# Other slot order in the first half; set 1 of the tokens turned by VectorE from 512-byte pieces

## The chip, the cores and the metric

The kernel runs on one core of one Trainium2 chip. The metric is device time in microseconds (us), the median of several runs of the same program. The kernel works in fp32 values with matmuls in the fp32r format.

## The reference

Input `A_u` is `[1, 2048, 576]` in fp32: 2048 tokens with 576 features. Cut to what matters:

```python
x  = A_u
xn = _layernorm(x)                       # per token
s  = S4D(xn)                             # long convolution over the tokens, per feature
def _B_ref(x, w1, b1, w2, b2):           # per token; d_ff = 4608
    y = _layernorm(x)
    h = _gelu(y @ w1 + b1)
    return h @ w2 + b2
g  = _silu(_B_ref(xn, ...))
return x + s * g
```

S4D builds a kernel K of length 2048 for each feature from sums of complex exponentials, convolves it with `xn` through a Fourier transform and adds `xn * D_skip`. The MLP (`_B_ref`) is nearly all of the arithmetic.

## The kernel before, in words

**Accuracy by halves.** A matmul takes fp32r operands. So each operand is split into a high part (the copy that ACT writes in fp32r) and a low part (the difference, that DVE subtracts), and a product is three matmuls: high by high, high by low, low by high. This holds for the tokens (`XH`, `XL`, and `XR` for the last 64 features, high and low in one tile), the weights (`w1h`, `w1l`, `w1r`, `w1s`, `w2h`, `w2l`) and the hidden values (`hh`, `hl`).

**Slots.** The 16 tiles of 128 tokens are worked in two halves of 8, and each half in two sets of 4 tiles (512 tokens). Tile b holds the tokens b, b + 16, b + 32 and so on. The 4608 hidden units are cut into 12 groups (`NG`) of 384. A slot is one group on one set: first layer (three pieces of 128 hidden units, 14 matmuls each, contracting over the features in four blocks of 128 and one of 64), Gelu on ACT, then the second layer (72 matmuls), whose results DVE adds into `acc` (line 573). There are 48 slots, and before the change they go: group 0 set 0, group 0 set 1, group 1 set 0, group 1 set 1 and so on, twice over, once for each half. The first slot has a first layer of its own (`first_layer1`).

**Weights.** `load_raw` brings the weights of a group in pieces into the tile `raw` through SP's queue, in the order of the list `PARTS`; `split_raw` splits a piece (ACT line 488, DVE line 485) and then issues the loads of the pieces that may take its room. There is one copy of the split weights of each layer, so the next group's `w1` is split while the last slot of the present group is in its second layer, and its `w2` while the next slot is in its first; `weigh_in` queues this, with times by which each piece is due.

**Tokens.** Each tile is normalised on DVE (`norms`: `stats`, `roots`, `recip`, `second`), and its tokens must be turned so that features lie on partitions. The first half does this on PE: `y_transpose` (line 413) transposes 128 x 128 blocks of a tile into PSUM, from which ACT takes the high part (417, 419) and DVE the low part (423, 425). Set 0 is turned ahead of slot 0, set 1 by `turn_lines(4, 1)` between slots 0 and 1. The second half stores its normalised tiles to the DRAM tensor `y_s` (line 388). `block_lines` then loads them back for one block of 128 features and 512 tokens at a time, in four DMAs on SP's queue of 32 partitions each, in pieces of 32 features (128 bytes, line 1231), so that one DVE transpose of 32 x 32 blocks (line 1236) puts features on partitions; ACT (1241) and DVE (1248) split the result.

**S4D.** Beside the MLP, DVE, ACT and POOL prepare S4D's tables; its matmuls (lines 869 to 1059) are put on PE between those of the MLP. The normalised tiles for it are stored to `xn_s` by POOL.

**What sets the order.** `Order` is a planner that runs while the program is traced. It keeps a clock for each engine, with a cost written into each step, and lines of steps that wait for marks of other steps (`need`, `mark`). Steps of the MLP are urgent and have times by which they are due; others go where the planner finds an engine free. `pin` fixes the order found on each engine, SP's queue among them. On the chip an engine keeps to this order and waits where an operand isn't there, whatever the planner had thought.

Of the kernel before, what the change touches and what calls it, by code (L numbers as in the profile page):

```python
# [9 lines left out]
F32 = mybir.dt.float32  # L10
# [8 lines left out]
P = 128  # L19
# [16 lines left out]
G = 3  # L36
# [6 lines left out]
def dve(n):  # L43
    return 0.075 + 0.00104 * n
# [168 lines left out]
def mixer_kernel(ctx, tc, u, log_a_real, a_imag, c_real, c_imag, log_dt, d_skip, w1, b1, w2, b2,  # L213
# [22 lines left out]
    y_s = dr.tile([8, P, D], F32, name="y_s")  # L236
# [114 lines left out]
    def norms(b0, n):  # L351
# [31 lines left out]
        def second(t, engine=nc.vector):  # L383
# [3 lines left out]
            if b0 >= 8:  # L387
                nc.sync.dma_start(dram(y_s, (b0 + t - 8) * P * D, [[D, 64], [64 * D, 2], [1, D]]), y)
            else:
                YT[b0 + t] = y  # L390
# [14 lines left out]
    def y_transpose(b0, tb, kb, q=None):  # L405
# [6 lines left out]
        def turn(i):  # L412
            nc.tensor.transpose(q[:n, i * P:(i + 1) * P], YT[b0 + i][:, kb * P:kb * P + n], idp)  # L413
# [24 lines left out]
    def load_raw(queue=nc.sync):  # L438
# [10 lines left out]
        elif i < KB:  # L449
            queue.dma_start(r, w1[i * P:(i + 1) * P, f])  # L450
        else:
            for e in range(2):
                queue.dma_start(r[e * 64:(e + 1) * 64], w1[KB * P:, f])
# [96 lines left out]
    def layer2(g, tb, j, terms, last, alone=False):  # L550
# [5 lines left out]
        c = slice(j * P, (j + 1) * P)  # L556
        if alone and terms[0][1]:
# [12 lines left out]
        def add(dh, n):  # L570
            o = acc[:, tb * 4 + j].rearrange("p (h d) -> p h d", h=2)[:, dh:dh + n]
            b = bias2.rearrange("p (h d) -> p h d", h=2)[:, dh:dh + n]
            nc.vector.tensor_add(o, q[:, dh:dh + n, :288], b if g == 0 else o)  # L573
# [616 lines left out]
    def norm_lines(b0, n=4):  # L1190
# [6 lines left out]
        for t in range(n):  # L1197
            nl["steps"].append(step("DVE", 0.6, lambda t=t: second(t), mark=("yn", b0 + t)))
            xl["steps"].append(step("POOL", 2.6, lambda t=t: first(t), need=[("yn", b0 + t)], mark=("xs", b0 + t)))
            wx["steps"].append(step(None, 5.0, lambda: None, need=[("xs", b0 + t)], mark=("xn", b0 + t)))  # L1200

    def turn_lines(b0, tb):
        x, xh, x2 = nl, nlh, nl2
        cell = {}

        def first(k0):
            for kb in (k0, k0 + 1):
                if kb <= KB:
                    cell[kb] = y_transpose(b0, tb, kb)
                    for i in range(4):  # L1210
                        cell[kb][0](i)
        M = lambda *a: ("turn", tb, b0) + a
        for ks in ((0, 1), (2, 3), (4,)):
            x["steps"].append(step("PE", 0.5 * len(ks), lambda k0=ks[0]: first(k0), cv=1,
                                   need=[M("l", 1)] if ks[0] == KB else (), mark=M("t", ks[0])))
            for kb in ks:
                xh["steps"].append(step("ACT", 0.6, lambda kb=kb: cell[kb][1](), need=[M("t", ks[0])], mark=M("h", kb)))
            for kb in ks:
                x2["steps"].append(step("DVE", 0.6, lambda kb=kb: cell[kb][2](), cv=-(kb == ks[-1]),
                                        need=[M("h", ks[-1])], mark=("x", tb) if kb == KB else M("l", kb)))  # L1220

    YB = []

    def block_lines():

        def load(tb, kb):
            if not YB:
                YB.extend(sb.tile([P, D], F32, name="row", bufs=NROW)[:, :TB] for _ in range(4))
            y = YB[(tb + kb) % 2]
            for q in range(4 if kb < KB else 2):  # L1230
                nc.sync.dma_start(y[32 * q:32 * q + 32].rearrange("p (b j) -> p b j", j=32), dram(
                    y_s, 4 * tb * P * D + kb * P + 32 * q, [[D, 32], [32 * D, NT], [1, 32]]))

        def blocks(tb, kb):
            n, k = P if kb < KB else 64, (tb + kb) % 2
            nc.vector.transpose(YB[2 + k][:n], YB[k][:n])

        def high(tb, kb):
            y = YB[2 + (tb + kb) % 2]
            if kb < KB:  # L1240
                nc.scalar.activation(XH[:, kb, tb], y, AF.Copy)
            else:
                nc.scalar.activation(XR[:64, tb], y[:64], AF.Copy)
# [308 lines left out]
```

## Time and profile before

| What | Value |
| --- | --- |
| Median of 3 runs | 1083.9 us (1082.99 to 1084.34) |
| The profiled execution's own time | 1082.74 us |
| Its span (first to last instruction) | 1081.0 us |
| Mean granted PE clock | 0.998 |
| PE busy | 1071.7 us, 99% |
| PE weight loads busy | 933.9 us, 86% |
| DVE busy | 947.9 us, 88% |
| ACT busy | 650.7 us, 60% |
| POOL busy | 199.1 us, 18% |
| DMA | 125.54 MB, mean 116 GB/s |

PE is TensorE's matmuls, PEld its weight loads, DVE is VectorE, ACT ScalarE, POOL GpSimd and SP SyncE, which issues DMAs. L413 is line 413 of the kernel. A row of a group gives line, engine, operation, the tiles written and read, shapes and count, then the busy us, the mean ns of one, the idle time of the engine ahead of them and what ended it. A row of the timeline gives start and length in us, engine, line, operation, tiles and count. Matmuls are pipelined, so the length of one contains part of its neighbours.

### The profile page before, as it was taken

What the parts mean: (1) busy time and instruction counts of PE and PEld (TensorE: products, weight loads), DVE (VectorE), ACT (ScalarE), POOL (GpSimd) and SP (SyncE); (2) the same over time, 40 slices, a digit from 0 to 9 for tenths busy, and PEclk for the clock granted to TensorE, in tenths of its full rate; (3) what the DMA queues carried; (4) which work ended last, traced back from release to release, by engine and by line L of the source; (5) the groups of instructions that cost most, each with busy time, mean ns of one, the idle gap of its engine ahead of it and who ended that gap; (6) DMA issues with size and microseconds to landing.
All of it is one profiled execution on the core that took longest, in us unless ns stands there. A gap on an engine that the chain in (4) does not pass through costs nothing.

```text
span 1081.0 us, 27198 instructions
## 1 busy us (share of the span) xinstructions
PE 1071.7 (99%) x11491; PEld 933.9 (86%) x11491; DVE 947.9 (88%) x1518; ACT 650.7 (60%) x974; POOL 199.1 (18%) x281
## 2 busy tenths in 40 slices
PE   9999999999999999999999999999999999999997
PEld 7989999889888888888888888888888887888896
DVE  7797878989999999999999999999999996677366
ACT  6558569767666665767756666576665754233333
POOL 6559342110000200002100010000100022110231
PEclk9999999999999999999999999999999999999999
DMA  7746455823225221455523433142312347332344
GB/s 236 229 140 190 163 186 196 229 71 113 72 71 110 65 80 55 112 94 129 144 59 100 82 86 88 33 124 55 97 53 76 115 85 237 111 111 88 89 156 117
DMA packets 136537, 125.54 MB, mean 116 GB/s; under 512 B 88156, under 2 KB 108096, under 8 KB 135392
## 3 DMA queue, kind: packets, MB, share of 16 engines
q1 hardware_dynamic: 120624, 76.44, 26.2%
q0 software_dynamic: 15040, 46.40, 13.8%
q8 instruction: 90, 1.47, 0.6%
q10 hardware_dynamic: 752, 0.97, 0.3%
q14 instruction: 31, 0.25, 0.1%
HBM read 95.52 MB, written 34.01 MB: 120 GB/s over the span
## 4 chain that ended last, share of the span: by engine, by line
PE 98%; DVE 1%; issue 1%; DMA 0%; ACT 0%; POOL 0%; ACTq 0%; POOLq 0%; DVEq 0%
PE mxa L508 22%; PE mxa L565 21%; PE mxb L565 21%; PE mxb L508 21%; PE cv L869 3%; PE cv L979 3%; PE cv L1032 2%; PE cv L941 2%; PE cv L1059 1%; DMA idp<-in_ident_dram 0%; PE mxa L523 0%; PE cv L413 0%; DVE A L646 0%; DVE row L386 0%; DVE acc L573 0%
## 5 line engine op out<-in xcount | busy, mean ns | idle before, releaser
L565 PE MATMUL mxa<-w2h,hh 128*128 128x288 f32 x573 | 171.3, 299 | 0.0
L565 PE MATMUL mxb<-w2h,hh 128*128 128x288 f32 x576 | 170.9, 297 | 0.0
L565 PE MATMUL mxb<-w2h,hl 128*128 128x288 f32 x576 | 170.0, 295 | 0.0
L565 PE MATMUL mxb<-w2l,hh 128*128 128x288 f32 x576 | 169.6, 294 | 0.0
L565 PE MATMUL mxa<-w2h,hl 128*128 128x288 f32 x573 | 169.1, 295 | 0.0
L565 PE MATMUL mxa<-w2l,hh 128*128 128x288 f32 x573 | 168.7, 294 | 0.0
L547 DVE TENSOR_TENSOR hl<-h,hh 128x512 fp32r<-128x512 f32 x144 | 99.4, 692 | 76.8 <-ACT hh L544 76.1
L541 ACT ACTIVATE h<-mxa,b1t 128x512 f32<-128x512 f32 x73 | 50.2, 690 | 126.3 <-PE mxa L508 121.7
L769 POOL DMA_DIRECT2D par<-par_s x36 | 27.3, 759 | 519.4 <-DVE mg L812 479.7
L565 PEld LDWEIGHTS mxa<-w2h,hh 128*128 128x128 f32 x573 | 107.6, 188 | 9.4 <-issue 6.3
L565 PEld LDWEIGHTS mxb<-w2h,hh 128*128 128x128 f32 x576 | 108.2, 188 | 4.9 <-issue 2.5
L565 PEld LDWEIGHTS mxb<-w2l,hh 128*128 128x128 f32 x576 | 108.1, 188 | 0.6
L565 PEld LDWEIGHTS mxa<-w2l,hh 128*128 128x128 f32 x573 | 107.6, 188 | 0.7
L565 PEld LDWEIGHTS mxb<-w2h,hl 128*128 128x128 f32 x576 | 108.1, 188 | 0.0
L565 PEld LDWEIGHTS mxa<-w2h,hl 128*128 128x128 f32 x573 | 107.5, 188 | 0.0
L541 ACT ACTIVATE h<-mxb,b1t 128x512 f32<-128x512 f32 x71 | 48.9, 689 | 76.9 <-PE mxb L508 76.1
L544 ACT ACTIVATE hh<-h 128x512 fp32r<-128x512 f32 x144 | 90.8, 632 | 4.0
L573 DVE TENSOR_TENSOR acc<-mxa,acc 128x576 f32<-128x576 f32 x88 | 65.4, 743 | 17.0 <-PE mxa L565 16.7
L508 PE MATMUL mxa<-XH,w1h 128*128 128x512 f32 x284 | 80.2, 404 | 0.0
L508 PE MATMUL mxb<-XH,w1h 128*128 128x512 f32 x280 | 77.1, 397 | 0.0
L508 PE MATMUL mxa<-XL,w1h 128*128 128x512 f32 x284 | 76.2, 390 | 0.0
L508 PE MATMUL mxa<-XH,w1l 128*128 128x512 f32 x284 | 76.0, 389 | 0.0
(231 smaller groups left out, 2420.8 us busy)
## 6 DMA issues: line engine op xcount, KB each, us to landing
raw<-in_B_w_dram SPq DMA_DIRECT2D x72, 288.0 KB, 3.3
raw<-in_B_w_dram SPq DMA_DIRECT2D x96, 192.0 KB, 2.9
par_s<-A POOLq DMA_DIRECT2D x8, 1080.0 KB, 5.9
par<-par_s POOLq DMA_DIRECT2D x36, 240.0 KB, 3.3
f2t<-f2q SPq DMA_DIRECT2D x24, 256.0 KB, 3.7
raw<-in_B_w_dram SPq DMA_DIRECT2D x48, 96.0 KB, 3.6
u_s<-in_A_u_dram POOLq DMA_DIRECT2D x16, 288.0 KB, 4.3
xc<-xn_s SPq DMA_DIRECT2D x48, 96.0 KB, 3.8
```

Source lines behind the costliest of these rows:

```text
L508: nc.tensor.matmul(q, a, b, start=j == 0, stop=j == len(ops) - 1)
L541: nc.scalar.activation(t, q, AF.Gelu_apprx_tanh, bias=b1t[:, g * G + i:g * G + i + 1], scale=1.0)
L544: LAST[0] = nc.scalar.activation(hh[:, i], t, AF.Copy)
L547: nc.vector.tensor_sub(hl[:, i], t, hh[:, i].bitcast(F32))
L565: nc.tensor.matmul(q[:, dh, :288], a[:, i, c], b[:, i, d], start=i == 0 and k == 0, stop=i == G - 1 and k == 2)
L573: nc.vector.tensor_add(o, q[:, dh:dh + n, :288], b if g == 0 else o)
L769: nc.gpsimd.dma_start(PAR[b].rearrange("p (g i) k -> p g (i k)", g=4), dram(par_s, (b // 6 * CH + b % 6 * 4) * NPAR, [[D * NPAR, P], [24 * ...
L869: nc.tensor.matmul(q[32 * g:32 * g + 32, i // 2, i % 2 * 64:i % 2 * 64 + 64], U[:, ri, 4 * g + i, :], v[:, ri, 4 * g + i, :], start=ri == ...
L941: nc.tensor.matmul(Q1ST[i, x][g // 2][64 * f:64 * f + 64, g % 2].rearrange(order), f1t[r].rearrange("p s k -> p (s k)"), rhs(r, f), start= ...
L979: nc.tensor.matmul(Q[i][32 * q:32 * q + 32, f, 2 * ri:2 * ri + 2], m[r, 4 * i + q, 32 * ri:32 * ri + 32], A2[r, 4 * p + 2 * i + q // 2, :, ...
L1032: nc.tensor.matmul(QI[q // 2][64 * f:64 * f + 64, q % 2, i], MAT["g2t", p + i // 2][r, i % 2, ri], YS[p + i // 2][0][r, i % 2, ri, f], sta ...
L1059: nc.tensor.matmul(Q[f][32 * e:32 * e + 32, t], g1t[r], A2[r, k:k + 2, 1].rearrange("p i d r -> p i r d"), start=True, stop=True, skip_gro ...
```

## The change

It has three parts.

1. **Order of the slots.** The first half starts with group 0 set 0, group 1 set 0, group 1 set 1, group 0 set 1, and goes on with group 2 as before. Group 0's weights are loaded and split a second time for the fourth slot. The first sum into `acc` of a set (with the bias) is found by a list of slots instead of by group 0.
2. **Set 1 of the first half is turned by DVE.** Its four tiles are stored to `y_s` as those of the second half are, and `block_lines(0)` takes the place of `turn_lines`. Its buffers lie in a tile that is free at that time, and its steps stand first in the planner's list. The loads of x from tile 8 on now come after the fourth block's load is issued.
3. **512-byte pieces.** In `block_lines`, for both halves, a load takes one tile of 128 tokens and 512 features, in pieces of 128 features. After the transpose of 32 x 32 blocks, partition p then holds the features 4p to 4p + 3, so that block k of the contraction is every fourth feature from k on. So that this holds everywhere, `w1`'s rows are loaded with a step of four, and the PE transposes of set 0 read the tile with a step of four elements. The last 64 features are loaded as before.

The diff, cut to its core:

```diff
-            if b0 >= 8:
-                nc.sync.dma_start(dram(y_s, (b0 + t - 8) * P * D, [[D, 64], [64 * D, 2], [1, D]]), y)
+            if b0 >= 4:
+                nc.sync.dma_start(dram(y_s, (b0 + t - 4) * P * D, [[D, 64], [64 * D, 2], [1, D]]), y)
...
         def turn(i):
-            nc.tensor.transpose(q[:n, i * P:(i + 1) * P], YT[b0 + i][:, kb * P:kb * P + n], idp)
+            y = YT[b0 + i]
+            y = y[:, kb:KB * P:KB] if kb < KB else y[:, KB * P:]
+            nc.tensor.transpose(q[:n, i * P:(i + 1) * P], y, idp)
...
-    for half in range(2):
-        for g in range(NG):
-            PARTS += [(half, g, 1, i) for i in range(KB + 1)] + [(half, g, 2, i) for i in range(G)]
+    SETS = [(0, (0,)), (1, (0, 1)), (0, (1,))] + [(g, (0, 1)) for g in list(range(2, NG)) + list(range(NG))]
+    SEQ = [(n, g, tb) for n, (g, tbs) in enumerate(SETS) for tb in tbs]
+    FIRST = (0, 2, 2 * NG, 2 * NG + 1)
+    for n, (g, _) in enumerate(SETS):
+        PARTS += [(n, g, 1, i) for i in range(KB + 1)] + [(n, g, 2, i) for i in range(G)]
...
-            queue.dma_start(r, w1[i * P:(i + 1) * P, f])
+            queue.dma_start(r, dram(w1, i * F + g * G * P, [[KB * F, P], [1, n]]))
...
+            if b0 == 4:
+                od.line()["steps"].append(step(None, 3.0, lambda: None, need=[("yn", b0 + t)], mark=("ys", b0 + t)))
...
-    def turn_lines(b0, tb):
...
+    def block_lines(half=1):
+
+        YB = []
+        if half == 0:
+            YB += [A2F[:, k:k + TB] for k in (2 * D, PT0 + 4 * D, PT0 + 4 * D + TB, PT0 + 4 * D + 2 * TB, 0, D)]
...
+        def source(tb, i):
+            return (0, 1, 4, 0, 5)[i] if half == 0 else (tb + i) % 2
+
+        def load(tb, i):
...
+            y = YB[source(tb, i)]
+            r = 4 * (tb + 1 if half else 0)
+            for q in range(4 if i < KB else 2):
+                if i < KB:
+                    nc.sync.dma_start(y[32 * q:32 * q + 32].rearrange("p (b d) -> p b d", b=4), dram(
+                        y_s, (r + i) * P * D + P * q, [[D, 32], [32 * D, 4], [1, P]]))
...
+        def blocks(tb, i):
+            k = (tb + i) % 2
+            x, y = YB[2 + k], YB[source(tb, i)]
+            if i < KB:
+                nc.vector.transpose(x.rearrange("p (k b t) -> p k b t", k=4, b=4),
+                                    y.rearrange("p (b j k) -> p k b j", k=4, b=4))
...
+        ks = [(tb, i) for tb in ((1,), range(2))[half] for i in range(KB + 1)]
         for n, k in enumerate(ks):
...
+            a, b, c, d = (yl, ml, mlh, ml2) if half else [od.line() for _ in range(4)]
+            early = half == 0
+            a["steps"].append(step(None, 3.5 + 1.5 * (k[1] == KB) if early else 5.5, lambda k=k: load(*k), mark=M("yl", *k),
+                                   need=[("ys", 4 + min(n, 3))] + ([M("yt", *ks[0])] if n == 3 else []) if early else [M("yt", *ks[n - 2])] if n > 1 else []))
...
+        if early:
+            d["steps"][-1]["mark"] = "x", 1
+            od.lines = od.lines[-20:] + od.lines[:-20]
...
-    turn_lines(4, 1)
+    block_lines(0)
...
-    nl["steps"].append(step(None, 7.0, rest_of_norms))
+    nl["steps"].append(step(None, 7.0, rest_of_norms, need=[("yl0", 1, 3)]))
...
-        g, tb = slot // 2 % NG, slot % 2
-        n = slot // 2
+        n, g, tb = SEQ[slot]
+        change = slot + 1 < NSLOT and SEQ[slot + 1][0] != n
```

More of the change, by code (lines that the diff above doesn't have):

```diff
@@ L235, in mixer_kernel @@
     u_s = dr.tile([P, NT, D], F32, name="u_s")
-    y_s = dr.tile([8, P, D], F32, name="y_s")
+    y_s = dr.tile([12, P, D], F32, name="y_s")
     g_s = dr.tile([8, P, D], F32, name="g_s")
@@ L556, in layer2 @@
         c = slice(j * P, (j + 1) * P)
+        first = turn[0] - 1 in FIRST
         if alone and terms[0][1]:
@@ L572, in add @@
             b = bias2.rearrange("p (h d) -> p h d", h=2)[:, dh:dh + n]
-            nc.vector.tensor_add(o, q[:, dh:dh + n, :288], b if g == 0 else o)
+            nc.vector.tensor_add(o, q[:, dh:dh + n, :288], b if first else o)
         return add
@@ L1458, in mixer_kernel @@
                 od.advance(od.t["PE"])
-                if pos == G - 1 and tb == 1 and slot + 1 < NSLOT:
+                if pos == G - 1 and change:
                     weigh_in(1)
@@ L1490, in mixer_kernel @@
                     od.urgent.append((od.t["PE"], chain))
-                if pos == NPOS - 1 and tb == 1 and slot + 1 < NSLOT:
+                if pos == NPOS - 1 and change:
                     weigh_in(2)
```

68 lines of the change are left out of this document (23 added, 45 removed).

## The prediction

> **What bounds the kernel now.** I read the page first (busy times, the chain that ended last), then PE's own waits, then PE's timeline where the change lies.
>
> ```profile
> span 1081.0 us, 27198 instructions
> PE 1071.7 (99%) x11491; PEld 933.9 (86%) x11491; DVE 947.9 (88%) x1518; ACT 650.7 (60%) x974; POOL 199.1 (18%) x281
> PE 98%; DVE 1%; issue 1%; DMA 0%; ACT 0%; POOL 0%; ACTq 0%; POOLq 0%; DVEq 0%
> ```
>
> ```profile
> PE mxa L1117 <- POOL XL L1111: 1.3, 1, 1.3
> PE cv L413 <- DMA idp<-in_ident_dram: 0.5, 1, 0.5
> ```
>
> PE sets the end throughout. These are the two longest of its three waits (us in total, times, longest); the third has 0.2 us, and all lie ahead of the end of start-up, 13 us. After that it waits for no engine. So the time follows the work on PE: a change gains what it takes off PE, and loses every wait that it puts in. DVE comes second with 88%.
>
> ```profile
> 22.64 0.29 PE L565 MATMUL mxa<-w2h,hh 128*128 128x288 f32 x1
> ...
> 29.79 2.26 PE L413 MATMUL cv<-idp,row 128*128 128x128 f32 x16
> 31.80 0.38 PE L565 MATMUL mxb<-w2h,hh 128*128 128x288 f32 x1
> 32.02 0.30 PE L565 MATMUL mxb<-w2l,hh 128*128 128x288 f32 x1
> ...
> 34.27 0.60 PE L413 MATMUL cv<-idp,row 128*64 128x128 f32 x4
> 34.62 1.17 PE L508 MATMUL mxa<-XH,w1h 128*128 128x512 f32 x4
> 35.63 1.07 PE L508 MATMUL mxa<-XL,w1h 128*128 128x512 f32 x4
> 36.54 1.07 PE L508 MATMUL mxa<-XH,w1l 128*128 128x512 f32 x4
> ...
> 44.24 0.29 PE L565 MATMUL mxb<-w2h,hh 128*128 128x288 f32 x1
> ...
> 53.76 1.09 PE L508 MATMUL mxb<-XH,w1h 128*128 128x512 f32 x4
> ```
>
> Matmuls overlap, so the price of one is the distance from its start to the next: 0.13 us in the second layer (44.24 to 53.76 for 72), 0.91 us for four of the first (35.63 to 36.54). A slot is 34.62 to 53.76, 19.1 us, of which the second layer takes 9.5.
>
> **What comes off PE.** The 20 transposes of set 1 go. Sixteen hold PE from 29.79 to 31.80, 2.01 us; the matmul behind them holds 0.22 instead of 0.13, so 0.09 more. Four hold 34.27 to 34.62, 0.35 us; the four matmuls behind them 1.01 instead of 0.91, 0.10 more. Sum 2.01 + 0.09 + 0.35 + 0.10 = **2.55 us**. All else stays on PE: 48 slots, only in another order.
>
> **What is added on the other engines.** Group 0's weights come twice in the first half, and set 1 is turned on DVE.
>
> ```profile
> L485 DVE TENSOR_TENSOR w2l<-raw,w2h 128x576 fp32r<-128x576 f32 x72 | 50.3, 748 | 1.8 <-ACT w2h L488 1.7
> L485 DVE TENSOR_TENSOR w1l<-raw,w1h 128x384 fp32r<-128x384 f32 x94 | 47.6, 556 | 0.0
> L1043 DVE STREAM_TRANSPOSE A<-A 128x512 f32<-128x512 f32 x36 | 22.8, 682 | 1.2 <-ACT A L1039 1.2
> L1236 DVE STREAM_TRANSPOSE row<-row 128x512 f32<-128x512 f32 x8 | 5.3, 686 | 0.0
> ```
>
> ```profile
> L488 ACT ACTIVATE w2h<-raw 128x576 fp32r<-128x576 f32 x72 | 44.8, 675 | 49.9 <-PE mxa L565 48.8 <-DMA raw<-in_B_w_dram 1.0
> L488 ACT ACTIVATE w1h<-raw 128x384 fp32r<-128x384 f32 x96 | 42.2, 509 | 0.1
> ```
>
> DVE: 5 w1 splits at 0.556 and 3 w2 splits at 0.748 are 5.0 us, 5 block transposes at 0.69 are 3.4: +8.4 us. The five high and five low parts of set 1 are there before and after. ACT: 5 at 0.509 and 3 at 0.675, +4.6 us. The new transposes read every fourth element, which no row does. Bounds: 0.68 (L1043 reads pairs from far apart and costs what the plain L1236 does) and twice that; I take 0.69, from the nearest row. At twice, DVE does 3.4 us more.
>
> Set 1's work runs in the gaps that DVE and ACT have in the first slots; the S4D work behind it moves back by up to 8.4 us and has room near the end (a stretch, then the busy us of PE, PE's weight loads, DVE, ACT and POOL, each with its number of instructions, the granted clock, DMA's share and GB/s):
>
> ```profile
> 920.00:940.00 20.00, 20.00 (x183) 16.92 (x182) 9.82 (x18) 5.21 (x10) 5.07 (x10) 1.00 0.28 80
> 30.00:40.00 10.00, 9.87 (x62) 8.71 (x61) 4.93 (x8) 7.07 (x10) 8.90 (x8) 1.00 0.72 267
> ```
>
> DVE idles 10.2 of the 20 us from 920 on with PE full, and 5.1 of the 10 us from 30 on: cost 0. Without that cover, 8.4 us of S4D would stand at the end. DMA gets 1.8 MB of weights (4 x 192 + 2 x 96 + 3 x 288 KB), 1.15 MB of stores to y_s and as much of block loads: 4.1 MB, some 15 us at the 267 GB/s of the second row. The loads of x from tile 8 on, 2.3 MB, move behind them.
>
> **The new deadlines.** Slot 0's second layer starts at 22.64 and, without transposes, ends 9.5 us later, at 32.2. Slot 1 is group 1 on set 0 from 32.2 to 51.3, with its second layer from 41.8. Set 1 is due at 51.3 instead of 34.6; w1 of group 1 at 32.2 instead of 53.8.
>
> ```profile
> 19.12 4.75 SPq L450 DMA_DIRECT2D raw<-in_B_w_dram  x4
> 23.92 1.13 SPq L453 DMA_DIRECT2D raw<-in_B_w_dram  x2
> ```
>
> ```profile
> L450 SPq DMA_DIRECT2D raw<-in_B_w_dram x96: 327/371/1058, 3.6 to 997.4; - x96
> DMA to landing us min/median/max: 2.3/2.9/5.0
> ```
>
> These are that w1's loads, issued by 25.05 and so landed by about 27.4 (28.9 to 29.5 if the last takes the longest time); its splits, 0.51 on ACT and 0.55 on DVE each, end by 31. That holds. The raw w2 of group 1 can be issued when these splits free the ring (29 to 31), lands 3 us later and is split by 38, due at 41.8: 4 us to spare, in which SP may stand at a wait for a store to y_s.
>
> The close one is set 1.
>
> ```profile
> 26.98 1.71 DVE L386 TENSOR_SCALAR row<-A,U 128x576 f32<-128x576 f32 x2
> ```
>
> ```profile
> L388 SPq DMA_DIRECT2D y_s<-row x8: 518/552/602, 59.4 to 81.3; - x8
> DMA to landing us min/median/max: 2.4/2.8/5.4
> ```
>
> ```profile
> L1231 SPq DMA_DIRECT2D row<-y_s x36: 302/488/1578, 452.7 to 529.5; - x36
> DMA to landing us min/median/max: 1.9/3.2/5.2
> ```
>
> The first tile's norm ends at 27.8, its store has landed at 30.6. From there SP issues three more stores (3 x 0.55), three w2 loads (1.0) and 18 block loads. Issue of a block load: 0.49 (L1231, up to 512 pieces of 128 B) or 0.37 (L450: as many pieces as the new 512-byte form, 128). I take 0.37 for the number of pieces: 30.6 + 1.7 + 1.0 + 6.7 = 40.0, the last one lands at 43.2, and transpose, high and low part (0.7 + 0.6 + 0.7) make set 1 ready at 45.2, **6 us ahead of slot 2**. At 0.49 it is 47.4. So set 1 itself is in time. But the wait stands on DVE, which works in a fixed order, and this is behind it:
>
> ```profile
> 45.83 0.69 DVE L547 TENSOR_TENSOR hl<-h,hh 128x512 fp32r<-128x512 f32 x1 [0.41 <-ACT hh L544]
> ```
>
> ```profile
> 46.88 0.29 PE L565 MATMUL mxb<-w2h,hl 128*128 128x288 f32 x1
> ```
>
> The low part of the slot's third hidden piece leaves DVE at 46.52, and the first matmul that reads it starts at 46.88: 0.36 us to spare, and its start is 1.59 us behind that of the second layer. In the new slot 1 this L547 is ready to start at 43.4 and must start by 43.7. If a transpose stands ahead of it in DVE's order and waits for its load, PE waits as long. By 0.37 us an issue the fourth block lands near 42.5, its transpose is done at 43.2, and the fifth needn't stand ahead: 0 us. By 0.49 the last transpose ends at 46.0: 2.3 us. I take 0, by the row with the same number of pieces.
>
> **Start-up.** The 20 transposes of set 0 now read rows of x with a step of four elements.
>
> ```profile
> L413 PEld LDWEIGHTS cv<-idp,row x36: 109/140/143, 9.7 to 34.5; 128*128 128x128 f32 x28, 128*64 128x64 f32 x8
> ```
>
> No weight load of before has such a step. Bounds: no change, and double (0.28). Fifteen of them come in the last 2 us ahead of the first real matmul, at 12.96, so double would be 15 x 0.14 = 2.1 us of delay. I take 0. The row can't tell; it is a rival. The Trainium skill speaks against the step here: SBUF — State Buffer, in the section on Door 1, has 16-byte lines of SBUF, where every access that goes to a new line pays; a step of four fp32 is a new line each time. It gives no price. By it D below happens, at up to 1083.5; L1043's pairs, two to a line, neither bear it out nor refute it.
>
> **Sum.** On the profiled execution's own time, 1082.74 (1.7 us around its span of 1081.0): 1082.74 - 2.55 = 1080.2. The median of the runs, 1083.9, is 1.2 above it; 1083.9 - 2.55 = 1081.35. I forecast **1081.4 us**.
>
> **The rivals.**
> - A, the forecast: 2.55 off PE and no new wait. 1081.4, own range 1080.4 to 1082.4 (where S4D falls among the slots changes PE's switches; "issue" is 1% of the chain). Chance 0.46.
> - B, a wait in place of the transposes: DVE stands at block loads ahead of slot 1's L547, PE waits 0.2 to 2.3 us. For it: 0.36 us to spare, and the code lets each block load of 3.5 us run beside the others, though SP issues them one after another. Against it: half of DVE is idle there. About 1081.4 + 1.4 = 1082.8. Chance 0.26.
> - C, slower: the block loads land late. The nearest burst:
>
> ```profile
> w<-in_A_u_dram SPq DMA_DIRECT2D x6, 288.0 KB, 7.1
> ```
>
> With 7.1 for store and load instead of 2.8 and 3.2, the fourth block comes at 42.5 + 8.2 = 50.7 and its transpose ends at 51.4, 7.7 us after the latest start of L547: 1081.4 + 7.7 = 1089.1. It decides from 4.7 us of waiting on: the 2.55, and the 0.2% of the time, 2.2 us, that a measurement of this kernel can just tell from no change. Against it: the x loads that made the burst now come later. Chance 0.13, part of it below that point.
> - D, the step in the weight loads costs: 1081.4 + 2.1 = 1083.5. Chance 0.10.
> - E, more gain than the transposes, by fewer switches of PE: 1080 or less. Chance 0.05.
>
> **How the numbers follow.** Faster by more than 2.2 us: three quarters of A, whose 2.55 is hardly above it, 0.34, E's 0.05 and 0.03 of B, together 0.42. Slower by more: 0.11 of C, 0.02 of B, 0.01 of D, together 0.14. The rest, 0.44, is no change. The range 1080.2 to 1085.8 takes in A, B, D and the lower part of C; it leaves out most of E and the upper part of C, together under 0.2.
>
> **What will show it.** Right: 20 L413 matmuls instead of 40, none after 13 us; no wait of PE for DVE or ACT in its list; slot 1 from 32.2, slot 2 at 51.3; DVE's busy time up by some 8 us. B: a PE wait at L565 near 42 to 45, with DVE idle at a block transpose for a DMA just before. C: the same at 4.7 us and more, landings above 5 us. D: the first L523 after 13.3 instead of 12.96, and L413's weight loads above 0.14. Wrong altogether: PE waiting for w1 at 32, or the end waiting for S4D.

## The result, and the profile after

| | Median | Range |
| --- | --- | --- |
| Kernel before (4 runs beside it) | 1083.46 us | 1082.99 to 1084.34 |
| Changed kernel (4 runs) | 1098.16 us | 1096.75 to 1099.16 |
| Ratio | 1.0134 | 95% interval 1.0118 to 1.0150 |

The change makes the kernel 14.7 us slower. The profiled execution took 1098.27 us with a span of 1096.4, 15.4 us more than the 1081.0 of before. From the page of the changed kernel (span, busy times, shares of the chain that ended last):

```profile
span 1096.4 us, 27197 instructions
PE 1075.0 (98%) x11471; PEld 933.7 (85%) x11471; DVE 958.7 (87%) x1531; ACT 645.0 (59%) x974; POOL 200.3 (18%) x281
PE 86%; DVE 5%; DMA 4%; issue 2%; SPq 1%; POOL 1%; ACT 1%; DVEq 0%; ACTq 0%; POOLq 0%
```

PE no longer makes up all of the chain: 14% of it now lies on DVE, DMAs and queues. PE's longest waits say where (line 570 is 565 of before, 551 is 547; the last of the three stood in the kernel before too):

```profile
PE mxb L570 <- DVE hl L551: 7.4, 5, 4.6
PE mxa L570 <- DVE hl L551: 2.2, 2, 1.7
PE mxa L1122 <- POOL XL L1116: 1.3, 1, 1.3
```

The longest lies in slot 1 (slots are counted from 0), whose second layer starts early and then stands. PE's timeline there, and DVE's from 33 us on:

```profile
44.77 0.29 PE L570 MATMUL mxb<-w2l,hh 128*128 128x288 f32 x1
49.70 0.40 PE L570 MATMUL mxb<-w2h,hl 128*128 128x288 f32 x1 [4.64 <-DVE hl L551]
```

```profile
33.61 1.06 DVE L386 TENSOR_SCALAR row<-A,U 128x576 f32<-128x576 f32 x2
...
46.63 1.08 DVE L1236 STREAM_TRANSPOSE A<-A 128x512 f32<-128x512 f32 x1 [5.01 <-DMA A<-y_s]
47.98 1.09 DVE L1236 STREAM_TRANSPOSE A<-A 128x512 f32<-128x512 f32 x1 [0.27 <-DMA A<-y_s]
49.00 0.65 DVE L551 TENSOR_TENSOR hl<-h,hh 128x512 fp32r<-128x512 f32 x1
```

Two block transposes stand in DVE's order ahead of the split (L551) that PE needs; the first of them waits 5.0 us for its load. The loads are late in the main because the norms are (e3 below takes that away): the first one starts at 33.61 instead of 26.98. ACT's timeline shows what stood ahead of the norms' square roots, and SP's what follows from them:

```profile
27.78 0.53 ACT L492 ACTIVATE w1h<-raw 128x384 fp32r<-128x384 f32 x1 [1.78 <-DMA raw<-in_B_w_dram]
29.75 0.53 ACT L492 ACTIVATE w1r<-raw 128x384 fp32r<-128x384 f32 x1 [1.44 <-DMA raw<-in_B_w_dram]
30.29 1.28 ACT L377 ACT_TABLE_LOAD   x1
```

```profile
34.42 1.25 SPq L388 DMA_DIRECT2D y_s<-row  x2
35.77 2.00 SPq L454 DMA_DIRECT2D raw<-in_B_w_dram  x3
37.87 1.18 SPq L388 DMA_DIRECT2D y_s<-row  x2
39.74 4.20 SPq L1226 DMA_DIRECT2D A<-y_s  x8
```

Group 1's `w1`, now due a slot earlier, is split ahead of the norms, and its loads are waited for. The stores and the block loads then go through SP one after another, and the eight loads issued from 39.74 on have their transposes at 46.63 and 47.98.

The same waits by stretch of time (columns as in the prediction: PE, PE's weight loads, DVE, ACT, POOL, granted clock, DMA's share, GB/s):

```profile
40.00:44.70 4.70, 4.70 (x30) 4.31 (x29) 1.57 (x2) 2.18 (x4) 4.35 (x3) 1.00 1.08 394
44.70:49.70 5.00, 0.36 (x3) 0.13 (x3) 2.80 (x4) 1.22 (x2) 3.75 (x4) 1.00 0.80 233
49.70:53.50 3.80, 3.80 (x17) 3.80 (x18) 2.93 (x4) 2.10 (x4) 0.00 (x0) 0.57 0.79 206
68.00:72.50 4.50, 2.10 (x10) 1.22 (x9) 4.37 (x11) 4.44 (x9) 0.00 (x0) 1.00 0.00 0
```

Ahead of the wait DMA's share (busy time of the 16 DMA engines, as the profile counts it) is 1.08; behind it PE ran for 3.8 us at a granted clock of 0.57. The last row is another wait, and DVE's timeline has its cause: a parameter of S4D whose load stands on SP behind the eight loads of x.

```profile
67.10 0.78 DVE L693 STREAM_TRANSPOSE A<-mg 128x576 f32<-128x576 f32 x1 [3.81 <-DMA mg<-in_A_C_imag_dram]
```

**Where the 15.4 us went.** From the distances between the starts of PE's matmuls, less the usual 0.13 or 0.23 us for each: 4.8 at 44.8 us and 1.6 of slow clock behind it; 0.6 at 55.7; 3.1 at 68 to 72; 2.6 at 150 to 173, while S4D's parameters (`par_s`, `par`) are late; 1.7 at 483 and 0.9 at 532, where DVE comes late from the second half's block transposes; 0.6 at 817; and 0.6 at the start (first L527 at 13.53 instead of 12.96). That is 16.5, less the 2.55 that came off PE, so 13.9; the other 1.5 I did not place. Of the 16.5, 10.7 lie in the first 72 us; the rest is small and scattered.

### The profile page after: what moved, and what is told of

Read it like the earlier page. It is cut to its first block, busy times and chain, and to the rows that moved or that the text cites. A ratio compares the mean times of both kernels' runs of the same rounds, so it can differ in the third digit from the quotient of the medians.

```text
span 1096.4 us, 27197 instructions
## 1 busy us (share of the span) xinstructions
PE 1075.0 (98%) x11471; PEld 933.7 (85%) x11471; DVE 958.7 (87%) x1531; ACT 645.0 (59%) x974; POOL 200.3 (18%) x281
## 4 chain that ended last, share of the span: by engine, by line
PE 86%; DVE 5%; DMA 4%; issue 2%; SPq 1%; POOL 1%; ACT 1%; DVEq 0%; ACTq 0%; POOLq 0%
PE mxa L570 19%; PE mxb L570 19%; PE mxb L512 18%; PE mxa L512 18%; PE cv L984 3%; PE cv L874 3%; PE cv L1037 2%; PE cv L946 2%; DMA par_s<-A 1%; DMA par<-par_s 1%; PE cv L1064 1%; DVE hl L551 1%; DMA mg<-in_A_C_imag_dram 0%; DMA y_s<-row 0%; DVE row L1236 0%
## 5 line engine op out<-in xcount | busy, mean ns | idle before, releaser
L551 DVE TENSOR_TENSOR hl<-h,hh 128x512 fp32r<-128x512 f32 x144 | 98.5, 685 | 69.1 <-ACT hh L548 68.6
L492 ACT ACTIVATE w2h<-raw 128x576 fp32r<-128x576 f32 x75 | 46.4, 674 | 58.3 <-PE mxa L570 48.9
```

Source lines behind the costliest of these rows:

```text
L492: nc.scalar.activation(h, r, AF.Copy)
L551: nc.vector.tensor_sub(hl[:, i], t, hh[:, i].bitcast(F32))
```

## The experiments

"Slot 1, 2, 3, last" in the table below is the start of the first Gelu (ACT) of that slot, the last one that of slot 45, less the same of the kernel before, in us. It says roughly how far PE's chain has fallen behind there; a Gelu that is late by ACT's own order counts too. "Span" is the profiled span less 1081.0. Each kernel was timed beside the kernel before (medians 1082.8 to 1083.5).

```
                       slot 1  slot 2  slot 3  last   span   median   ratio (95% interval)
changed kernel          -2.7     3.5     8.3   15.6   15.4   1098.16  1.0134 (1.0118, 1.0150)
e1_order_only           -2.9     3.3     2.8    6.8    6.6   1089.97  1.0065 (1.0050, 1.0080)
e2_pieces_only           0.3    -0.1     0.6    1.5    1.3   1084.36  1.0011 (1.0001, 1.0020)
e3_norms_first           7.3    15.0    17.1   16.4   16.3   1098.98  1.0139 (1.0124, 1.0154)
e4_one_slot_later       -2.9     5.1     9.7   16.4   16.6   1099.64  1.0148 (1.0128, 1.0168)
e5_real_costs           -3.0     4.5     6.1    6.3   20.9   1103.58  1.0193 (1.0178, 1.0208)
e6_real_later           -2.8    -0.3     0.9    0.2   11.9   1094.80  1.0112 (1.0097, 1.0127)
e7_order_x_first        -2.5     6.4     7.6   13.2   13.0   1096.55  1.0122 (1.0105, 1.0139)
e8_real_later_x_last    -2.6     0.5     1.0   -2.5    9.0   1091.72  1.0083 (1.0066, 1.0100)
e9_end_early            -2.6    -0.1     1.0   -2.8   12.2   1094.97  1.0110 (1.0094, 1.0127)
e10_order_x_last        -3.3    -1.7    -0.4   12.5   14.3   1096.32  1.0126 (1.0111, 1.0142)
e11_after_x_last        -3.4     3.3     4.8   17.6   19.3   1101.69  1.0172 (1.0157, 1.0188)
e12_params_later        -3.4    -2.3    -1.9   -5.4    9.4   1092.57  1.0092 (1.0077, 1.0107)
c0_end_and_tables       -1.9     2.6     3.3    6.6    8.1   1090.89  1.0069 (1.0055, 1.0083)
c1_pool_lows            -2.8     2.2     3.3   19.4   19.2   1101.88  1.0172 (1.0158, 1.0186)
c2_old_due_pool         -3.0     6.4     8.0   18.8   18.6   1101.05  1.0171 (1.0155, 1.0187)
b1_before_same_end      -0.4    -0.9    -0.4    6.6    6.4   1089.27  1.0056 (1.0043, 1.0070)
b2_before_loads_late     0.0    -1.6     0.0    1.7    1.4   1084.56  1.0010 (1.0000, 1.0019)
b3_before_dve_10us       0.0    -0.4     0.3    0.7    0.4   1083.58  1.0002 (0.9991, 1.0012)
```

My theory T: the planner orders VectorE by costs for set 1's stores, loads and transposes that are too low, so a transpose that has to wait for its load stands ahead of a split that PE needs. Rivals: O, the slot order itself; P, the strided pieces; L, set 1 is simply late, whatever the order.

### The order alone, and the pieces alone

`e1_order_only` is the kernel before with

```diff
+    SETS = [(0, (0,)), (1, (0, 1)), (0, (1,))] + [(g, (0, 1)) for g in list(range(2, NG)) + list(range(NG))]
```

and what goes with it; `e2_pieces_only` is the changed kernel with the old order (`SETS = [(g, (0, 1)) ...]`) and `turn_lines(4, 1)` back in place of `block_lines(0)`.

> The kernel before with the new slot order alone (group 0 set 0, group 1 both sets, group 0 set 1); set 1 is still turned by TensorE from SBUF and the second half keeps its small pieces. Theory T (what costs is the late landing of set 1's blocks on VectorE's queue): 1081 to 1086 us, no wait over 1.5 us in the first five slots; one more fetch and split of group 0's weights costs nothing. Theory O (the order itself, with group 0's weights fetched twice and group 1's wanted at once, is what costs): 1090 us or more, with waits of 3 us or more at the first layer's matmuls of slots 1 to 3.

> The changed kernel with the old slot order and set 1 of the first half turned by TensorE: what is left of the change is the 512-byte pieces in the second half, and weight loads and transposes in steps of 16 bytes at the start. Theory T: 0.6 us at the start and up to 3 us in the second half, so 1084 to 1087 us, no wait over 1.5 us before 60 us. Theory P (the strided operands are what costs): 1090 us or more.

The pieces cost 1.2 us in all (1.0011): P falls. The order alone costs 7 us, more than T and a shade less than O expected, with waits under O's 3 us, so neither holds as written. Its early loss is one wait of 2.4 us at 60 us, in slot 2's first layer (the expectations count it as slot 3); later waits make up 3.8 us more. DVE's timeline shows what lies behind the early one:

```profile
PE mxb L510 <- ACT h L543: 3.4, 2, 2.4
```

```profile
59.23 0.78 DVE L691 STREAM_TRANSPOSE A<-mg 128x576 f32<-128x576 f32 x1 [4.13 <-DMA mg<-in_A_C_imag_dram]
```

It is the same parameter load as in the changed kernel, here too on SP right behind the loads of x. That made a theory M, of its own: what stands on SP behind the eight token loads comes late.

### The norms first, the costs as measured, set 1 a slot later

`e3_norms_first`, `e5_real_costs` and `e4_one_slot_later` are the changed kernel with, in turn, the edits below (cut). e3 has the same `late=` on the reciprocal and the second steps of the norms. e5 also gives each load of set 1 2.0 us on SP, one after another, and 4.5 us to land, and each transpose 1.1 us.

```diff
-        nl["steps"].append(step("ACT", 0.5, roots, tbl="sqrt"))
+        nl["steps"].append(step("ACT", 0.5, roots, tbl="sqrt", late=20.0 if b0 == 4 else 0.0))
...
-                od.line()["steps"].append(step(None, 3.0, lambda: None, need=[("yn", b0 + t)], mark=("ys", b0 + t)))
+                od.line()["steps"].append(step(None, 5.5, lambda: None, need=[("yn", b0 + t)], mark=("ys", b0 + t)))
...
-    SETS = [(0, (0,)), (1, (0, 1)), (0, (1,))] + ...
+    SETS = [(0, (0,)), (1, (0,)), (2, (0, 1)), (0, (1,)), (1, (1,))] + ...
```

> The changed kernel with one edit: the roots, the reciprocal and the second steps of set 1's norms are put ahead of the splits of group 1's first-layer weights in the planner's order, as they were before the change. Theory T: the first normalized tile is done near 28 us instead of 33.6, the blocks land 4 to 6 us earlier, the 4.8 us wait of slot 1 falls below 1.5 us and the clock stays at 1.00: 1084 to 1092 us. Rival C (the small pieces land late whenever they are issued, because of what shares the DMA engines at that time): the first tile is done earlier but the loads' landings grow by the same, the wait stays over 3 us, 1094 to 1099 us.

> The changed kernel, only the planner's costs for set 1's stores, loads and block transposes set to what the trace of after shows (store 5.5 us from end of the norm, 2.0 us of issue for each load one after another on SP, 4.5 us landing, 1.1 us a transpose). Theory T (VectorE's order, made with too low costs, puts a transpose that has to wait ahead of the split that TensorE needs): the wait of slot 1 falls below 0.5 us; in its place TensorE waits 3 to 8 us at slot 2 for set 1, once: 1085 to 1096 us. Rival L (set 1 is simply late, whatever VectorE's order): the whole is as after, 1096 to 1100 us.

> The changed kernel with the order group 0 set 0, group 1 set 0, group 2 both sets, group 0 set 1, group 1 set 1, so that set 1 is wanted one slot later (near 70 us). The planner's costs are as in the change. Theory T (VectorE's order with too low costs): the block transposes still stand ahead of the splits of slots 1 to 2, so a wait of 3 us or more for a hidden split is left; 1090 us or more. Rival L (set 1 is simply late for its slot): the wait of slot 1 is gone, 1086 us or less.

PE's two longest waits in e3, and ACT's row where the first one ends:

```profile
PE mxa L512 <- ACT h L545: 7.0, 1, 7.0
PE mxb L570 <- DVE w2l L489: 4.1, 1, 4.1
```

```profile
44.21 0.63 ACT L1250 ACTIVATE XH<-A 128x512 fp32r<-128x512 f32 x1 [15.87 <-DVE A L1236]
```

With the norms first, the first tile is done at 29.5 (28 was expected) instead of 34.2, but the blocks are turned only 3.5 us earlier (43.10 instead of 46.63), and now the first block's high part stands in ACT's order ahead of slot 1's first Gelu. ACT idles 15.9 us and PE loses more than before. So the expectation of T was missed: earlier norms don't help while the order is made with low costs, and the wait only moves to another instruction. The total lies in the range of e3's rival C, but of the 4.7 us that the first tile came earlier only 1.2 were lost again on the way to the transposes, where C had said all.

e4 kept its wait, as T expected, and rival L falls for slot 1:

```profile
PE mxb L570 <- DVE hl L551: 7.2, 4, 4.4
```

In e5 the costs alone were changed. The wait of slot 1 is gone (0.5 us are left, at an `acc` of the slot's end) and its place is taken by one wait for set 1 at slot 2, at 51.9 us:

```profile
PE mxb L512 <- ACT XH L1250: 5.9, 1, 5.9
```

That is T's reading of slot 1, and also L's of slot 2: in this slot order set 1 is late there even when nothing stands in its way at slot 1 (5.9 us here, 6.9 in c2 below). But the total is 1103.6 and not at most 1096, because the end after PE's last matmul grew from 6.9 to 18.0 us, which no theory had.

### Real costs and a slot later; where the loads of x stand

`e6_real_later` joins e5 and e4. `e8_real_later_x_last` adds `at=60.0` to the step of the token loads, `e11_after_x_last` is the changed kernel with that alone. `e7_order_x_first` and `e10_order_x_last` are e1 with those loads at 29 and 60 us:

```diff
-    nl["steps"].append(step(None, 7.0, rest_of_norms))
+    nl["steps"].append(step(None, 7.0, rest_of_norms, at=60.0))
```

> The same later order, with the planner's costs for set 1's stores, loads and transposes as measured (those of the run with real costs). Theory T: neither a wait for a split behind a transpose nor one for set 1: PE loses under 2 us before 90 us. What is left is what the later plan does elsewhere (loads of parameters behind the loads of tokens on SP): 1081 to 1090 us. Rival L: the same 1081 to 1086. If more than 4 us are lost before 90 us, both are wrong.

> The later order with real costs, and the token loads not before 60 us, so behind the loads of the third and fourth parameter on SP. Theory M: VectorE waits for no parameter for more than 1 us; PE loses under 1 us before 90 us; 1081 to 1087 us. If the loads' landing is set by all that is under way, whatever its order on SP, the wait stays: as the run with the later order and real costs, within 1 us.

> The order alone (first run of this study) with one edit: the loads of the other 8 tiles of tokens go out at 29 us, as in the kernel before, and not after set 1's turn, where they stood on SP right ahead of the loads of the third parameter (mg), which VectorE then waited for (4.1 us from 55.1). Theory M (a transpose that waits on VectorE for a load queued behind the token loads is what the order alone costs): the wait of 2.6 us at slot 3 is gone, and PE is within 1 us of the kernel before at 70 us; the total falls by 2.5 to 6 us, to 1084 to 1087.5. Rival O (the order's extra weights): the wait stays, 1089 to 1091.

> The order alone, with the token loads not before 60 us in the plan, so behind the loads of the third and fourth parameter and of the weights. Theory M (what the order alone costs in the first slots is whatever stands on SP right behind the 8 token loads): neither the wait of 2.6 us at slot 3 (order alone) nor that of 4.6 at 44 (token loads at 29): PE within 1 us of the kernel before at slot 5, 1081 to 1086 us. Rival O (the order's extra weights make the loads late wherever the tokens stand): 2 us or more are lost before 70 us again, 1088 or more.

> The changed kernel with the token loads not before 60 us in the plan and nothing else. Theory M: the wait of slot 1 stays (4 to 5 us at 44.8, and the slow clock behind it), the 3.1 us at 68 to 72 go away: 1092 to 1096 us. If all losses have one source, they stay: 1098.

In the first slots T and M are borne out in the main. The long waits are gone in e6 and e8, which are within 1.0 us of the kernel before at slot 3; but by the distances between its matmuls PE still loses about 3 us ahead of 90 us, in pieces under 0.8 us, where T had expected under 2 for e6 and M under 1 for e8. e10 (the order alone) is 0.4 us ahead of the kernel before, so the order's additional weights cost nothing there. In e11 the wait of slot 1 stays and that at 68 us is gone, as expected. e7 misses M's expectation of 1 us at 70 us: the old wait is gone, and with the token loads early it is the weights behind them that wait (4.4 us on PE). ACT's row there:

```profile
44.41 0.68 ACT L490 ACTIVATE w2h<-raw 128x576 fp32r<-128x576 f32 x1 [6.71 <-DMA raw<-in_B_w_dram]
```

But all five totals were missed. e8 has PE 2.5 us ahead at its last slots and still takes 1091.7. e10 and e11 lose 7.6 and 6.2 us in one wait near 880 us, behind a load of the end work (`row<-g_s`, for which DVE stands 7.9 and 6.4 us). Something late in the kernel had become a bound.

### The end

`e9_end_early` is e8 with `END = 1003.0` for 1020.0; `e12_params_later` is e9 with

```diff
-  for k, t in ((0, 28.0), (2, 42.0), (3, 48.0), (1, 54.0))]
+  for k, t in ((0, 28.0), (2, 50.0), (3, 56.0), (1, 62.0))]
```

and the token loads at 68.

> The run with the later order, real costs and the token loads last, with one number changed: the time by which the plan spreads the last S4D pieces, 1020 to 1003. Its 15 us after TensorE's last matmul (7 in the kernel before) came from the last chunk's stores, issued at 1030.9 against 1014.2. Theory Q (the plan's clock runs ahead of the chip's, so the end work starts too late): the stores go out 14 to 17 us earlier, the end after the last matmul is 7 us again, and the total is 1082 to 1085 us. Rival (the end work waits for VectorE, which has more to do): the end stays above 12 us, 1089 to 1092.

> As the run with the earlier end time, with the parameter loads 8 us later in the plan (50, 56 and 62 us) and the token loads at 68. If the 2.2 us that PE still loses at 49 to 65 us come from these loads between the weights and the blocks on SP: under 1 us is left, and the total is 1 to 2 us below that run. If not, the same within 1 us.

Theory Q falls: with the earlier end time e9's last S4D stores go out later than e8's (1041.9 instead of 1035.0), and its span is 3.2 us longer. e12, which keeps that number, has 0.7 us of PE's loss left, as expected. It is the clearest run of the study. Its whole list of PE's waits:

```profile
PE mxa L1122 <- POOL XL L1116: 1.3, 1, 1.3
PE mxa L527 <- ACT XH L419: 0.2, 1, 0.2
PE mxb L512 <- ACT XH L1250: 0.2, 1, 0.2
```

PE's last matmul ends at 1072.2 us, 1.7 ahead of the 1073.9 of before: the 2.55 us are there, nearly whole. But the span is 9.4 us longer, and its chain ends in a load of the end work:

```profile
1074.33 4.63 DMA row<-g_s
```

That work is three rounds of loading, adding up and storing, one after another on POOL's queue, and it needs the last S4D results (`s_s`). From the start of their last store to the end of the last round it is 43 us in e12, 46 in the changed kernel and 49 in the kernel before. The results come from S4D's tables, 36 in all, that DVE makes. First and last start of a table's product and of a store, in the kernel before, the changed one, and e12:

```profile
L823 DVE TENSOR_TENSOR U<-w,mg x36: 1180/1218/1226, 186.1 to 891.6; 128x1024 f32<-128x1024 f32 x36
...
L1070 POOL DMA_DIRECT2D s_s<-ys x24: 582/582/585, 369.7 to 1018.2; - x24
```

```profile
L828 DVE TENSOR_TENSOR U<-w,mg x36: 1184/1219/1228, 197.5 to 925.5; 128x1024 f32<-128x1024 f32 x36
...
L1075 POOL DMA_DIRECT2D s_s<-ys x24: 585/585/600, 395.0 to 1037.5; - x24
```

```profile
L828 DVE TENSOR_TENSOR U<-w,mg x36: 1181/1218/1227, 205.3 to 927.8; 128x1024 f32<-128x1024 f32 x36
...
L1075 POOL DMA_DIRECT2D s_s<-ys x24: 582/582/592, 389.6 to 1039.3; - x24
```

The first table is 11 and 19 us later than before, the last one 34 and 36, the last store 19 and 21. They don't catch up. DVE has little time free between 200 and 900 us; two of the kernel before's stretches there:

```profile
200.00:300.00 100.00, 100.00 (x1041) 87.41 (x1040) 94.92 (x137) 69.62 (x95) 9.95 (x15) 1.00 0.37 104
300.00:400.00 100.00, 100.00 (x1328) 84.89 (x1334) 97.06 (x153) 64.60 (x95) 8.38 (x13) 1.00 0.35 88
```

DVE works 95 and 97 of 100 us. That this is why the lag stays is argued here, and c0 and c1 below speak for it; why it grows from 11 to 34 us on the way is not shown. So there is a second chain, S4D's, nearly as long as PE's. In the changed kernel it is hidden, because PE is late by as much (its last store is at 1037.5, like that of e12); take PE's waits away, as e12 does, and it sets the end, 9.4 us later than before. Some 3 us of the 9.4 may come from the end time alone, by e9 against e8.

### What makes S4D late

Four runs tried the S4D chain. c0 is e12 with half of the token loads at 44 us, the tables not held back (`ALONE = 0.0`) and the end work's loads planned at 9.0 us instead of 14.5 and 10.0; c1 takes the low parts of the turned blocks on GpSimd; c2 is c1 in the order of the change under study; b1 is the kernel before with c0's three numbers of the end.

```diff
-            nc.vector.tensor_sub(lo, y, h.bitcast(F32))
+            (nc.gpsimd if i < KB else nc.vector).tensor_sub(lo, y, h.bitcast(F32))
```

> As the run with the parameters later, and three edits for the S4D chain: 4 of the 8 token loads at 44 us in the plan and 4 at 62 (so that their norms come earlier), the matmuls of the tables no longer held back 3 us, and the end work's loads planned at 9 us instead of 14.5 and 10. Theory S: the last table stands some 4 slots' thirds (28 us) earlier in VectorE's order, so the last S4D stores go out near 1010 to 1020 us instead of 1035; the end after the last matmul is 7 to 9 us; the total is 1080.5 to 1084 us if PE loses under 2 us in the first slots. Rival (badly planned end alone): the stores stay near 1030, and only the planned waits give 4 to 6 us: 1086 to 1089.

> The same, and the low parts of the turned blocks are taken by GpSimd instead of VectorE (12 subtractions of 128x512, 0.68 us each on VectorE, so 8 us off VectorE). Theory S: VectorE has 8 us more, so the last table is no later than in the run without this edit, and the total within -2 to +1 us of it. Rival: GpSimd's queue makes set 1 late for its slot, or takes longer than 1.4 us each: 1 to 4 us slower than that run.

> The same as the run with GpSimd, but with the order of the change under study (set 1 due at slot 2, two weight sets fewer). TensorE waits 4 to 8 us at slot 2 for set 1 as in the run with real costs; its S4D chain is the earliest in VectorE's order of all these, so the end is 7 us: 1085 to 1090 us. If the S4D chain alone set the time, it would be the fastest: below 1083.

> The kernel before with the three numbers of the end alone (the end time 1003, the tables not held back, the end loads planned at 9 us). Its S4D chain has slack at the end (TensorE's last matmul sets its time), so no change is expected: 1081.5 to 1084.5 us. A gain of over 2 us would mean that what the other runs of this call gain is not the change's.

c0 brings the end after PE's last matmul to 7.3 us, as theory S expected, and the last S4D stores to 1024.8 (S: 1010 to 1020); but PE is 3.3 us behind at slot 3 again (2.0 of it in one wait at 59.9), and 6.6 at the end, so the total is 1090.9. b1 was meant as a control and shows that c0's three numbers of the end do harm by themselves. DVE stands 4.0 us for one of the end loads, which are now planned at 9 us, and PE behind it, 3.1 us, with 1.5 more of slow clock:

```profile
PE mxb L565 <- DVE acc L573: 3.1, 1, 3.1
```

The same numbers also bring b1's last S4D stores to 1007.7, so c0, c1 and c2 are to be compared with b1 there. The totals of c1 and c2, which have the same wait (3.3 and 3.8 us near 1025 to 1030), don't say much on GpSimd or on the due time. Their S4D chains do. c1 differs from c0 in the low parts alone, 8 us of work less on DVE, and its last table starts at 914.5 instead of 924.0 and its last stores at 1020.2 instead of 1024.8, though PE is later: DVE's time does bear on this chain. c2, in the slot order of the change, starts its first table at 182.4 and its last at 892.0 (b1: 185.7 and 902.4), so this order does not make the tables late by itself. No run beats the kernel before.

The last two took the kernel before and did one thing alone: the loads late (`at=68.0` for the tokens, 50, 56 and 62 for the parameters), or 15 subtractions of 128x512 more on DVE. The latter write to a tile that holds S4D's parameters, so that kernel's output isn't the reference's; its instructions are the kernel before's and the 15.

> The kernel before, with the token loads at 68 us and the parameter loads at 50, 56 and 62 us in the plan (30 to 36 and 36 to 54 us before), nothing else. If the late loads make the S4D chain late: the last S4D stores go out 10 to 25 us later than 1018, the end after the last matmul is 12 us or more, 1088 to 1095 us. If the loads have that much slack (the plan puts the tables at the same places of VectorE's order as before): 1082 to 1085 us.

> The kernel before, with 15 subtractions of 128x512 added on VectorE (0.69 us each, 10.3 us; their result goes into a spare tile), offered to the plan from 36 us on, one each 3 us, nothing else. By the prediction's step (added VectorE work lies in idle time of the first 200 us): 1082 to 1085 us. If VectorE's time is the bound of the S4D chain already here: the last S4D stores 8 to 12 us later, 1084 to 1092 us.

Neither makes S4D late: the last stores of b2 and b3 start at 1019.9 and 1018.9.

```profile
L1070 POOL DMA_DIRECT2D s_s<-ys x24: 582/582/585, 371.7 to 1019.9; - x24
```

```profile
L1070 POOL DMA_DIRECT2D s_s<-ys x24: 585/585/587, 370.4 to 1018.9; - x24
```

Token loads 33 us later, with parameter loads 9 to 14 us later, cost at most 0.2%, and 10 us of DVE work at that place nothing that can be measured. What makes the first table late in the new order is thus not shown. One guess is both together, by way of POOL's queue: the parameters of the first tables are loaded by POOL in order behind its share of the norms of tiles 8 to 15, whose last store goes out at 94 us in the kernel before, 134 in b2, 139 in the changed kernel and 163 in e12, and the first such load at 135, 140, 158 and 171. But c2 speaks against it: its last such store goes out at 141 and its first load at 152, near those of the changed kernel, and its first table is 3.7 us earlier than in the kernel before. No run moved this queue alone, and the cause stays open.

## Why the prediction was wrong

I had said 1081.4 us (1080.2 to 1085.8); it is 1098.2. By its own steps:

- **What comes off PE**: right. Slot 1 is 1.9 to 3.4 us early in every run with the new order that doesn't put the norms first (2.7 in the changed kernel), and e12 ends PE's work 1.7 us early. The term of 2.55 is borne out.
- **What is added on the other engines**: counts right, one size wrong. DVE's busy time rose by 10.8 us, where I had 8.4. The strided transpose takes 1.09 us where I took 0.69 (bounds 0.68 and double), and I counted only set 1's: the second half's eight read with the same step, 3.3 us more in all:

```profile
L1236 DVE STREAM_TRANSPOSE row<-row x8: 1057/1093/1101, 478.7 to 544.1; 128x512 f32<-128x512 f32 x8
L1236 DVE STREAM_TRANSPOSE A<-A x4: 1082/1090/1109, 46.6 to 54.6; 128x512 f32<-128x512 f32 x4
```

  The cover for +8.4 us of DVE holds as far as pure work goes (b3). What I left out is DVE standing: in 40 to 70 us it works 18.7 of 30 us, against 28.0 before, and the work missing there is mostly the norms of later tiles (lines 371 to 386: 10.2 us before, 2.4 here), whose tokens S4D takes.

```profile
40.00:70.00 30.00, 24.32 (x129) 21.23 (x128) 18.74 (x30) 13.23 (x20) 8.10 (x6) 0.94 0.84 237
```

```profile
40.00:70.00 30.00, 30.00 (x185) 27.61 (x184) 28.05 (x54) 18.93 (x29) 13.40 (x9) 1.00 0.72 199
```

- **The new deadlines: the step that failed.** The sum rests on set 1 being ready 6 us ahead of slot 2, with no transpose that waits ahead of slot 1's split; neither held. I put the norms where they stood in the old order (first tile done at 27.8), though I had moved group 1's `w1` to a due time of 32.2 on the same ACT and DVE; they were done from 34.2 on. I took landings from quiet times, 2.8 us for a store and 3.2 for a load, and 0.37 us of SP for a load's issue. In this stretch, with DMA at a share of 1.08 just ahead of the wait, the four stores landed after 4.8 to 5.3 us, the block loads after 2.2 to 5.1 (median 3.9), and an issue took 0.46. I let the block loads go out in one run; SP's order has weights between them, so that the fourth block, landed at 42.5 in my sum, was only loaded and turned here:

```profile
50.36 2.57 SPq L1226 DMA_DIRECT2D A<-y_s  x4
54.60 1.09 DVE L1236 STREAM_TRANSPOSE A<-A 128x512 f32<-128x512 f32 x1 [1.24 <-DMA A<-y_s]
```

  And I asked when the data would be there, but for DVE's order I reasoned about where the transposes "need" to stand; they stand where the planner's costs put them, 3.0 us for a store and 3.5 for loads side by side. In e5, where these costs alone are changed, the wait of slot 1 is gone, and PE waits 5.9 us for set 1 at slot 2 instead.
- **The rivals**: it went by C's mechanism at B's place, with DVE at a block transpose and PE at L565's successor at 44.8. C's price for that wait was 7.7 and it is 4.8. I gave it 0.13, and neither B nor C had what came behind: 1.6 us of slow clock, 3.1 of the parameter load on SP behind the tokens, and the scattered rest. Against C I had said that the loads of x now come later; that took them away from the blocks and put them ahead of `mg`.
- **Start-up**: D's mechanism is seen, its size isn't. The strided weight load has a median of 0.208 us, against 0.140:

```profile
L415 PEld LDWEIGHTS cv<-idp,row x16: 123/208/220, 10.1 to 12.7; 128*128 128x128 f32 x12, 128*64 128x64 f32 x4
```

  It overlaps the matmuls: from the first transpose to the first real matmul it is 3.39 us in the changed kernel (10.14 to 13.53) and in e2 (9.65 to 13.04), and 3.20 in the kernel before (9.76 to 12.96). So the step costs 0.19 us, where D had up to 2.1. The other 0.38 of the 0.57 us in the changed kernel is a later start, with a longer wait for `idp` (1.0 instead of 0.5), which differs from run to run. The Trainium skill's rule of 16-byte lines (SBUF — State Buffer, the section on Door 1) agrees in direction: reads of one element per line cost 1.09 against 0.69 us in the transpose and 0.21 against 0.14 in the weight load.
- **"The end waiting for S4D"** stood among what would make the prediction wrong altogether, with no price. In the changed kernel itself PE sets the end, but S4D's chain is the next bound: e12, in another slot order, has nearly all of the gain on PE and is 9.8 us slower than the kernel before.

## What to carry to other kernels

Where an order is fixed ahead of time, a step that is moved or added must be costed as the chip will run it, with its queue's serial issue and the landing times of that busy stretch: an engine that keeps order turns one late load into a wait for everything behind it. Before counting on an engine's idle time as cover, look at its busy share stretch by stretch to the end: at 95 to 97% for 700 us, an engine at 88% overall can be a second critical chain, whose late start was not made up here. And take the first wait away in an experiment before believing in the gain behind it: here that showed the gain on PE nearly whole, and another bound, 9 us later, right behind it.

## What the runs showed of the hardware

The granted clock of TensorE falls after a wait. After the 4.8 us of the changed kernel it was 0.57 over 3.8 us; after 6.1 us in e5 and 3.3 in b1 it was 0.50 over the next 3 us or so, which cost 1.7 and 1.5 us more. In all the runs, each of the 14 waits of 3.0 us and more after start-up is followed by such a stretch, which by the distances between matmuls cost 1.5 to 2.9 us beyond the wait's own length. Below that there is no sharp limit: after the wait of 2.6 us in slot 2 of e1 the clock stayed at 1.00; after one of 2.2 us in c1 near 531 us it fell (1.0 us more), and after one of 1.7 us in e4 at 70 us it was 0.50 over the next 3.4 us. The Trainium skill says as much of long waits (TensorE: Matmul & The Clock Gate, the part on the HAM clock gate: an idle window of about 3.4 us, which runs freely, brings the clock to half), and these traces agree in size; but waits shorter than that window, of 1.7 to 3.3 us, brought it down here too. I had left this out of the prices of B and C.
